# A linear-attention recurrence and an MLP in one instruction stream: a new order of MLP pieces, narrowings and joins

## The chip, the cores and the metric

The kernel runs on one core of one Trainium2 chip. The metric is the device time of one execution in microseconds (us), the median of several runs. Inputs come from and outputs go to HBM.

## The reference

For batch 4, 8 heads, 768 tokens and head size 48, a state of 48 x 48 per head is carried over the tokens (delta rule); then an MLP follows on the 3072 tokens with 384 features:

```python
k_n = k / (norm(k) + 1e-6)
for t in range(S):
    y[:, :, t] = einsum('bhd,bhde->bhe', q[:, :, t], state)
    v_old = einsum('bhde,bhd->bhe', state, kt)
    state = state + bt * einsum('bhd,bhe->bhde', kt, vt - v_old)
x = y.transpose(0, 2, 1, 3).reshape(B * S, H * D)      # 3072 x 384
h = x @ w_in                                            # 384 x 2048
out = (h * sigmoid(h)) @ w_out                          # 2048 x 384
```

The two MLP weights are float64 in HBM and are narrowed to fp32 on the chip with bit operations.

## The kernel before, in words

The 768 tokens are cut into six chunks (c = 0 to 5) of 128, each into two halves of 64 tokens (hf), and the 32 heads into two groups (g). Inside a chunk the recurrence becomes small dense algebra:

- *Scores* (`score`, L530): per head the products k k^T and k q^T within a half, evacuated by ACT and masked by DVE. Their diagonal 32 x 32 blocks go to HBM and come back turned (`block_out` L104, `block_in` L583), so that each of 128 partitions has one block.
- *Inversion* (`invert`, L628 and L633): on DVE, 31 steps per chunk, the triangular factor of all 128 blocks at once. Chunk 0 has its own form (`invert_first`, then `corner`, `turned`, `straight`, `merge_half` on PE, called "the joins", L718 to L807).
- *Factors out*: for chunks 2 to 5 through HBM (`low`, `up`, then xe and xi). For chunk 1 `put_up` (L602) turns the blocks on DVE in place: the first transpose (L606) writes xe, the second (L608) up, and copies make xi of it.
- *Solve* (`solve`): `merge` twice (py and px, L783) joins the 32 x 32 factors to 64 x 64; `keys` (ph, L829) subtracts the old state's part from v; `inner` (pz, L841) applies the factor; `old` (pyc, L909) and `new` (L922) give the outputs; `update` (pu, L861, and L868 on DVE) the next state. The outputs are gathered into xT, some of it by DMA (`move`, L902).
- *MLP*: `hidden` (phid, L1049) with Silu on ACT (L1059) out of two PSUM banks, m0 and m1. For chunk 0 `project` (po, L1084) multiplies by w_out. For the others `combine` (px, py, L1156) does so with sums of quarters of w_out and of the Silu's results (`sum_w` L1120, `sum_g` L1138).
- *Narrowing* (`narrow`, L232 to L245): per piece of 256 rows or columns of a weight, two instructions on ACT ("begin"), then two on DVE, the second with an addition on POOL behind it. w_in has eight pieces (in0 to in7), w_out eight (out0 to out7). The raw float64 data come by DMA (`fetch_w_out`, L306); each of these transfers waits, with `depth`, for the last but one ahead of it on SP's queue.

Every engine runs its instructions in the order in which the program issues them (`pin`), and all loads and stores are in one line on SP (`in_line`). The order is written by hand. For chunks 0 and 1 it is a string of words that `script` reads: `s` one step of `solve`, `j` steps of chunk 0's second joins, `r` one MLP piece (`run`: the next step of `pieces`, after the weight that it needs has been narrowed), `f` one step of a narrowing, `b` the begin of the next one, `p` a step of `prepare` (scores of chunk 1), `i` a step of `invert`, `w3` the load of w_out's raw piece 3, `z` a scaling of v on POOL (`size`), `v` load_v(1), `t` a step of `sum_w`, `m` of the key lengths of chunk 2, `c` all that is left of chunk 0's MLP and then chunk 1's MLP as the next pieces. A piece of `hidden` is three matmuls (six records of PE), one of `project` two, one of `combine` four. For chunks 2 to 5 a loop runs `go(solving)` and then so many pieces from a list.

In the old string chunk 0 has 64 pieces, r1 to r64 below: 16 of hidden(0, 0), 16 of hidden(0, 1), 32 of project.

Of the kernel before, what the change touches and what calls it, by code (L numbers as in the profile page):

```python
# [19 lines left out]
def kernel(  # L20
# [10 lines left out]
    nc = tc.nc  # L31
    B, H, S, D = q.shape
# [4 lines left out]
    NCH = S // C  # L37
# [3 lines left out]
    T = 32  # L41
# [29 lines left out]
    def behind(later, earlier, how=NoSync):  # L71

        tc.add_manual_dep(
            later.ins, earlier.ins.name,
            mybir.DependencyInfo(how, mybir.DependencyReason.DATA), reason="order",
        )
# [3 lines left out]
    def pin(op):  # L80

        engine = op.ins.engine
        if engine in pins:
            behind(op, pins[engine])
        pins[engine] = op
        return op
# [23 lines left out]
    def together(*parts):  # L110
        for _ in zip_longest(*parts):
            pass
# [52 lines left out]
    def in_blocks(c):  # L165

        return 1 < c < NCH
# [142 lines left out]
    def narrow_w_out(i):  # L310
# [14 lines left out]
        out=above[0:W], in_=above[0:W], pattern=[[1, W]], compare_op=ALU.is_gt, fill=0.0,  # L325
# [3 lines left out]
        out=above[W:P], in_=above[W:P], pattern=[[1, W]], compare_op=ALU.is_gt, fill=0.0,  # L329
# [214 lines left out]
    def by_act(to, of):  # L544
        return pin(nc.scalar.copy(to, of))  # L545
# [41 lines left out]
    xes = {}  # L587
# [14 lines left out]
    def put_up(x):  # L602

        both = work.tile([P, BH, T], FP32, name="xe_y", tag="g", bufs=1)
        xes[1], ys[1] = both[:], both[:].rearrange("p (g h) t -> p g h t", g=2)
        pin(nc.vector.transpose(out=both[:].rearrange("p n s -> p s n"), in_=x))  # L606
        up = work.tile([P, BH, T], FP32, name="up_1", tag="x", bufs=1)[:]
        pin(nc.vector.transpose(out=up.rearrange("p n t -> p t n"), in_=x.rearrange("p s t -> p t s")))  # L608
        for j in (1, 3, 0, 2):
            rows, cols = slice(T * j, T * (j + 1)), slice(T * (j % 2), T * (j % 2) + T)  # L610
            for g in range(2):
                of = up[rows, HH * g : HH * (g + 1)]
                if j % 2 == 1 and g == 1:
                    by_act(crossed[T * (4 - j) : T * (5 - j)], of)
                (by_dve if j % 2 == 1 and g == 0 else by_pool if j % 2 == 0 and g == 0 else by_act)(xis[g][rows, :, cols], of)
# [42 lines left out]
    Q, ys = T // 2, {}  # L658
# [177 lines left out]
    def inner(c, g, hf, room=CC):  # L836

        pz = bank(room, "pz")
        for u, p, e, n, _, _ in of_heads():
            rows = on(e, hf, g)  # L840
            yield pin(nc.tensor.matmul(  # L841
                pz[rows, n * D : (n + 1) * D], lhsT=xis[g][rows, u * H + 2 * p + e, :],
                rhs=vfs[c][rows, hf, g * HB + u, p, :], start=True, stop=True,
            ))
        to = zbuf[:, g * HB : (g + 1) * HB, hf, :, 0:D]
        if c == 0 and hf == 0:
            by = (by_act, by_dve) if g == 0 else (by_dve, by_act)
            at = slab[:, g * HB * NP * 2 * D + D :][:, 0 : HB * NP * 2 * D]
            by[0](at.rearrange("p (n w) -> p n w", w=2 * D)[:, :, 0:D], pz[:, 0:DM].rearrange("p (n d) -> p n d", d=D))
            by[1](to, by_heads(pz))  # L850
        else:
            by_act(to, by_heads(pz))
# [23 lines left out]
    def first_outputs(g):  # L876

        pys = [bank(A, f"py{e}") for e in range(2)]
        for u in range(HB):
            for a in range(NKT):  # L880
                for n in range(2):
                    for half in range(2):
                        f = P * a + W * half
                        h = f // D + n
                        p, e = h // 2, h % 2
                        at = ((g * HB + u) * NP + p) * 2 * D + D + f - D * h
                        pin(nc.tensor.matmul(
                            pys[e][HALVES[half], C * a + W * u : C * a + W * (u + 1)],
                            lhsT=slab[on(e, 0, g), at : at + W], rhs=aps[0, g][1][on(e, 0, g), u, h, :],
                            start=True, stop=True,  # L890
                        ))
        xT, half = x_half(0, g, 0)
        to = xT[:, :, half]
        even, odd = (py[:, 0 : NKT * C].rearrange("p (a t) -> p a t", a=NKT) for py in pys)
        by_act(to, even)
        pin(nc.vector.tensor_tensor(out=to, in0=to, in1=odd, op=ALU.add))
# [64 lines left out]
    def copy_out():  # L961
        together(copies.pop(0))
# [18 lines left out]
    def solve(c):  # L981

        if c == 0:
            together(inner(0, 0, 0, CC))
            together(inner(0, 1, 0, M))
            yield
            first_outputs(0)
            yield
            first_outputs(1)
            yield  # L990
            together(update(0, 0, 0), update(0, 1, 0))
            yield
            together(keys(0, 0, 1), keys(0, 1, 1))
            yield
            together(inner(0, 0, 1), old(0, 0, 1))
            yield
            together(inner(0, 1, 1), old(0, 1, 1))
            yield
            together(update(0, 0, 1), update(0, 1, 1))
            yield  # L1000
            together(new(0, 0, 1), new(0, 1, 1))
            copy_out()
            copy_out()
            move()
            yield
            return
        together(merge(c, 0, False), merge(c, 1, False))
        yield
        together(keys(c, 0, 0), keys(c, 1, 0))
        yield  # L1010
        together(merge(c, 0, True), merge(c, 1, True))
        yield
        for hf in range(2):
            if hf == 1:
                together(keys(c, 0, 1), keys(c, 1, 1))
                if c > 1:
                    follow(c)
                yield
            for g in range(2):
                together(inner(c, g, hf), old(c, g, hf))  # L1020
            if hf == 1:
                if c == 1:
                    follow(c)
                load_v(c + 1)
            yield
            made(c, hf)
            yield
            copy_out()
            if hf == 0:
                yield  # L1030
# [348 lines left out]
    corner, turned, straight = next(inv)  # L1379
# [38 lines left out]
    def run(n=1):  # L1418

        for _ in range(n):  # L1420
            name = next(needed, None)
            if name is not None:
                until(name)
            go(pieces)
            begin_soon()
# [121 lines left out]
                pieces = chained(feed_forward(1, 0), feed_forward(1, 1))  # L1547

    for text in (
        "s f s f T f q T s q T j5 j4 j8 j8 f j5 f q r T j20 j5 j8 j4 j16 j5 j4 b r q r f j4 j4 f W7 r b j4 f2 j4 j4 j32 r f e j6 j6 b j8 j4 f j4 j20 f j4 r j4 j99 l h f2 b l s w2 f r2 l p r s l w3 r p r l p f l2 f l3 b l f l2 s l f l p l3 r l3 s l f l r l2 p f s2 l2 H f l4 f r2 f p2 v l g G r i p i p f r i r i2 r i r i b l i r f r i r b r2 i b b b i2 r2 i2 f b i5 r6 f r f r i2 r2 f r i r f r f i4 f i b r2 i3 b f b f r i r i f k r f r z i b r s r2 t z s b r2 b s m2 r5 t f t m f t m2 r s t m r b s b m r m2 s r m r m r c m2 s m r m t b m2 s m2 b m f m2 t r t m3 r m s m",  # L1550
    ):
        script(text)
    for c in range(1, NCH):
        if c > 1:
            solving = solve(c)
            for n in range(9):
                go(solving)
                run(((2, 2, 2, 2, 1, 1, 2, 2, 2), (2, 2, 2, 1, 1, 2, 2, 2, 2))[c == NCH - 1][n])
                if n == 5:
                    pieces = chained(pieces, feed_forward(c, 0), feed_forward(c, 1))  # L1560
        assert next(solving, 0) == 0
        go(long_2, 99)
        if c + 1 < NCH:
            ready = prepare(c + 1)
            for _ in range(3 if c == 1 else 2):
                go(ready)
                run(2)
            step = block_steps(c + 1)
            go(ready)
            run(8 if c > 1 else 6)  # L1570
            for n, _ in enumerate(invert(c + 1, step)):
                run(int(n % 4 != 3 and n != 24))
                if n == 3:
                    load_k(c + 2)
                    if in_blocks(c + 2):
                        load_blocks(k, c + 2, ALL)
            after = lengths(c + 2) if c + 2 < NCH else iter(())
            for _ in range({1: 8, NCH - 2: 10}.get(c, 10)):
                run()
                go(after, 4)  # L1580
            go(after, 99)
# [31 lines left out]
```

## Time and profile before

| | us |
|---|---|
| median of 3 runs (639.11 to 640.27) | 639.91 |
| the profiled execution | 646.08 |
| its span | 644.3 |
| PE busy in it | 623.5 |
| DVE, ACT, POOL busy | 401.2, 217.2, 94.3 |

PE is TensorE (matmuls; PEld its weight loads), DVE VectorE, ACT ScalarE, POOL GpSimd, SP the queue that issues DMAs. L1049 is line 1049 of the kernel. In the lists "x6" counts instruction records; an fp32 matmul gives two. Some records of matmuls are missing in a trace. A row of the chain of waits has the start, the length and what ran. A row of a timeline has the start, the time to the end of the last of the group, the engine, the line, the operation and the tiles, and in brackets the idle time ahead of it with the releaser. PEclk is the granted clock of PE as a share of the full one.

### The profile page before, as it was taken

To read this page: it belongs to the slowest core of one execution; us is meant where nothing else is said; L and a number is where in the kernel's file an instruction comes from. 1 tells how busy PE (TensorE), PEld (TensorE's weight loads), DVE (VectorE), ACT (ScalarE), POOL (GpSimd) and SP (SyncE) were. 2 spreads that over 40 slices of the span, in tenths; PEclk is the share of its full clock that TensorE was granted. 3 is DMA by queue.
4 is the path that set the end of the run, shared out by engine and by line. 5 is a ranking of instruction groups with operands and counts; after the bars stand their busy time and mean duration, and the time that the engine had idled before them with its cause. 6 is when DMAs were issued, how large, how long until landed. Compare 5 with 4: busy or idle time off the path is not lost.

```text
span 644.3 us, 21893 instructions
## 1 busy us (share of the span) xinstructions
PE 623.5 (97%) x9642; PEld 550.1 (85%) x9642; DVE 401.2 (62%) x917; ACT 217.2 (34%) x512; POOL 94.3 (15%) x96
## 2 busy tenths in 40 slices
PE   6879999999999999999999999999999999999997
PEld 4677787756789988999989989989989989889997
DVE  5845688988865986563987563987464974212112
ACT  2655656151342122451122451122451122441120
POOL 5332630237011020010020010020001000000000
PEclk9759799999999999999999999999999999999999
DMA  9755445170278433268434268334173033100101
GB/s 190 164 141 163 146 97 132 50 148 3 58 150 145 62 85 50 54 133 136 70 79 55 47 137 138 69 79 56 26 154 76 9 79 48 40 14 1 25 0 25
DMA packets 141695, 53.69 MB, mean 83 GB/s; under 512 B 113296, under 2 KB 135056, under 8 KB 141600
## 3 DMA queue, kind: packets, MB, share of 16 engines
q1 hardware_dynamic: 141264, 52.14, 40.2%
q8 instruction: 76, 1.25, 0.8%
q10 hardware_dynamic: 336, 0.15, 0.1%
q14 instruction: 19, 0.16, 0.1%
HBM read 39.62 MB, written 10.49 MB: 78 GB/s over the span
## 4 chain that ended last, share of the span: by engine, by line
PE 92%; DMA 2%; issue 2%; DVE 1%; ACT 1%; SPq 1%; POOL 0%; DVEq 0%; POOLq 0%
PE phid L1049 39%; PE px L1156 16%; PE py L1156 12%; PE po L1084 7%; PE pa L530 3%; PE pz L841 2%; PE ph L829 2%; PE pyc L922 2%; PE pu L861 2%; PE pyc L909 2%; PE pt L501 1%; DMA kb<-in_k_dram 1%; DMA xT<-part 1%; PE px L783 1%; PE py L783 1%
## 5 line engine op out<-in xcount | busy, mean ns | idle before, releaser
L1049 PE MATMUL phid<-xT,w_in 128*128 128x256 f32 x1152 | 259.6, 383 | 2.5 <-DMA xT<-part 1.5
L1049 PEld LDWEIGHTS phid<-xT,w_in 128*128 128x128 f32 x1152 | 217.2, 191 | 33.6 <-issue 4.1
L1059 ACT ACTIVATE gT<-phid 128x512 f32<-128x512 f32 x88 | 52.6, 598 | 147.1 <-PE phid L1049 138.5
L628 DVE SCALAR_TENSOR_TENSOR rank<-g,step,x 128x31 f32<-128x31 f32 (+15 forms) x124 | 49.7, 401 | 36.9 <-DMA g<-blocks 33.4
L1138 DVE TENSOR_TENSOR sums_of_g<-gT 128x384 f32<-128x384 f32 (+1 forms) x60 | 29.8, 516 | 56.5 <-ACT gT L1059 46.0
L1156 PE MATMUL py<-w_out,sums_of_g 128*128 128x192 f32 x320 | 56.8, 329 | 0.0
L1156 PE MATMUL px<-sums_of_w,sums_of_g 128*128 128x192 f32 x320 | 56.6, 329 | 0.0
L1156 PEld LDWEIGHTS px<-sums_of_w,sums_of_g 128*128 128x128 f32 x320 | 52.2, 190 | 0.5
L1156 PEld LDWEIGHTS py<-w_out,sums_of_g 128*128 128x128 f32 x320 | 52.2, 190 | 0.4
L633 DVE TENSOR_TENSOR x<-x,rank 128x31 f32<-128x31 f32 (+15 forms) x124 | 42.5, 343 | 4.3
L468 POOL TENSOR_TENSOR vf<-vf,n_slot 128x768 f32<-128x768 f32 x10 | 14.9, 1490 | 167.9 <-DMA vf<-in_v_dram 121.8
L868 DVE TENSOR_TENSOR state<-state,pu 48x384 f32<-48x384 f32 x44 | 24.3, 552 | 21.9 <-PE pu L861 20.9
L545 ACT COPY xT<-pyc 48x128 f32<-48x128 f32 (+2 forms) x126 | 32.7, 260 | 1.7
L489 DVE STREAM_TRANSPOSE kq<-stage 128x512 f32<-128x512 f32 x28 | 28.2, 1112 | 3.9 <-DMA stage<-in_q_dram 3.8
L1156 PE MATMUL px<-sums_of_w,gT 128*128 128x192 f32 x160 | 28.4, 329 | 0.0
L1156 PE MATMUL py<-w_out,gT 128*128 128x192 f32 x160 | 28.4, 329 | 0.0
L1156 PE MATMUL px<-w_out,gT 128*128 128x192 f32 x160 | 28.0, 327 | 0.0
L841 PEld LDWEIGHTS pz<-vf,xi 64*64 64x64 f32 x768 | 25.2, 142 | 3.2 <-issue 2.6
L551 POOL COPY g<-x 64x256 f32<-64x256 f32 x4 | 5.0, 1242 | 152.5 <-DVE x L636 152.5
L1156 PEld LDWEIGHTS px<-w_out,gT 128*128 128x128 f32 x160 | 26.4, 190 | 0.6
L841 PE MATMUL pz<-vf,xi 64*64 64x48 f32 x768 | 26.9, 226 | 0.0
L1156 PEld LDWEIGHTS py<-w_out,gT 128*128 128x128 f32 x160 | 26.1, 190 | 0.3
(197 smaller groups left out, 831.1 us busy)
## 6 DMA issues: line engine op xcount, KB each, us to landing
vf<-in_v_dram SPq DMA_DIRECT2D x48, 96.0 KB, 3.1
out_dram<-o SPq DMA_DIRECT2D x42, 96.0 KB, 2.2
w_out<-in_moe_w_in_dram SPq DMA_DIRECT2D x12, 256.0 KB, 3.5
sums_of_w<-in_moe_w_out_dram SPq DMA_DIRECT2D x8, 384.0 KB, 4.4
blocks<-ap SPq DMA_DIRECT2D x40, 64.0 KB, 1.9
g<-blocks SPq DMA_DIRECT2D x5, 512.0 KB, 3.7
kb<-in_k_dram SPq DMA_DIRECT2D x12, 192.0 KB, 4.4
kb<-in_k_dram SPq DMA_DIRECT2D x24, 96.0 KB, 4.5
```

The lines of the kernel that those rows point to most:

```text
L489: pin(nc.vector.transpose(out=kqs[c, b][:, :, j, :].rearrange("p a (i m) -> p a m i", i=T), in_=src.rearrange("p a (m d) -> p a m d", d=D) ...
L530: pin(nc.tensor.matmul(pa[e][half, p * n * W : (p + 1) * n * W], lhsT=kq[rows, p, 0, half], rhs=kq[rows, p, js[0] : js[-1] + 1, half], sta ...
L545: return pin(nc.scalar.copy(to, of))
L628: pin(nc.vector.scalar_tensor_tensor(out=tv, in0=g[:, 0:m, m : m + 1].to_broadcast([P, m, n]), scalar=step[:, m : m + 1], in1=x[:, m : m + ...
L633: yield pin(nc.vector.tensor_tensor(out=x[:, 0:m, m:T], in0=x[:, 0:m, m:T], in1=tv, op=ALU.add))
L841: yield pin(nc.tensor.matmul(pz[rows, n * D : (n + 1) * D], lhsT=xis[g][rows, u * H + 2 * p + e, :], rhs=vfs[c][rows, hf, g * HB + u, p, : ...
L868: pin(nc.vector.tensor_tensor(out=to, in0=to, in1=by_heads(pu[of]), op=ALU.add))
L1049: pin(nc.tensor.matmul(ph[:, j * GT : (j + 1) * GT], lhsT=w_in[:, a, (2 * f + j) * P : (2 * f + j + 1) * P], rhs=xTs[c, hf][:, a, :], star ...
L1059: pin(nc.scalar.activation(out=hidden_of(c, hf, f), in_=ph[:], func=ACTF.Silu, scale=-0.5 if in_blocks(c) else 0.5))
L1084: pin(nc.tensor.matmul(pos[i][:, 0:DM], lhsT=hidden_of(0, hf, f // 2)[:, at : at + C], rhs=w_outs[f // HFF][:, f % HFF, :], start=(f == 0) ...
L1138: pin(nc.vector.tensor_tensor(out=sums_of_g[:, k, fs], in0=of[0], in1=of[1], op=op))
L1156: pin(nc.tensor.matmul(to, lhsT=at, rhs=quarter(f, *b) if isinstance(b, tuple) else sums_of_w[b][:, f], start=start and f == 0, stop=f == ...
```

## The change

Four things change:

1. `put_up`: the first transpose of chunk 1 writes its result contiguously; xes[1] becomes a view of it with the heads innermost, so that the merge's matmul reads its moving operand with a stride of 32 elements.
2. `solve`: the first merge and the first keys are one step in chunks 1, 2 and 4; in 3 and 5 they stay two.
3. The string: an `r` inside the joins ahead of merge_half(1), one ahead of chunk 0's update (the fourth `s`) with a `b` moved behind it, one `r` fewer behind the update and one fewer between the second and third score; `w3` moved from behind the fifth `s` to ahead of `v`, behind the xT moves; two `r` gathered ahead of the first inversion steps; `z` (the second) ahead of the merge; `c` behind the keys of chunk 1's second half; two `r` fewer behind it.
4. The loop: lists of pieces by chunk (eight entries where the row is shared), and 7 pieces for 6 ahead of chunk 2's inversion.

```diff
     def put_up(x):
         both = work.tile([P, BH, T], FP32, name="xe_y", tag="g", bufs=1)
-        xes[1], ys[1] = both[:], both[:].rearrange("p (g h) t -> p g h t", g=2)
-        pin(nc.vector.transpose(out=both[:].rearrange("p n s -> p s n"), in_=x))
+        turned = both[:].rearrange("p n t -> p (n t)").rearrange("p (s n) -> p s n", s=T)
+        xes[1], ys[1] = turned.rearrange("p s n -> p n s"), both[:].rearrange("p (g h) t -> p g h t", g=2)
+        pin(nc.vector.transpose(out=turned, in_=x))
...
         together(merge(c, 0, False), merge(c, 1, False))
-        yield
+        if c in (3, NCH - 1):
+            yield
         together(keys(c, 0, 0), keys(c, 1, 0))
...
-  j4 j4 f j4 j20 f j4 r j4 j99 l h f2 b l s w2 f r2 l p r s l w3 r p r l p f
+  j4 j4 f j4 j4 r j16 f j4 r j4 j99 l h f2 r l s w2 f r b l p r s l r p l p f
...
-  f r2 f p2 v l g G r i p i p f r i r i2 r i r i b
+  f r2 f p2 w3 v l g G r i p i p r2 f i i2 r i r i b
...
-  k r f r z i b r s r2 t z s b r2 b s m2
+  k r f r z i b z r s r2 t b r2 b s m2
...
-  s r m r m r c m2 s m r m t b m2 s m2 b m f m2 t r t m3 r m s m
+  s r m r m r m2 s c m t b m2 s m2 b m f m2 t r t m3 m s m
...
             solving = solve(c)
-            for n in range(9):
+            counts = {
+                2: (4, 3, 2, 1, 1, 2, 2, 2), 3: (2, 2, 2, 2, 1, 1, 2, 2, 2),
+                4: (2, 4, 2, 1, 1, 2, 2, 2), 5: (2, 2, 2, 1, 1, 2, 2, 2, 2),
+            }[c]
+            for n, count in enumerate(counts):
                 go(solving)
-                run(((2, 2, 2, 2, 1, 1, 2, 2, 2), (2, 2, 2, 1, 1, 2, 2, 2, 2))[c == NCH - 1][n])
-                if n == 5:
+                run(count)
+                if n == len(counts) - 4:
                     pieces = chained(pieces, feed_forward(c, 0), feed_forward(c, 1))
...
-            run(8 if c > 1 else 6)
+            run(8 if c > 1 else 7)
```

The lines of the string are shown as the stretches that differ, with their words in the kernel's order.

More of the change, by code (lines that the diff above doesn't have):

```diff
@@ L1549 @@
     for text in (
-        "s f s f T f q T s q T j5 j4 j8 j8 f j5 f q r T j20 j5 j8 j4 j16 j5 j4 b r q r f j4 j4 f W7 r b j4 f2 j4 j4 j32 r f e j6 j6 b j8 j4 f j4 j20 f j4 r j4 j99 l h f2 b l s w2 f r2 l p r s l w3 r p r l p f l2 f l3 b l f l2 s l f l p l3 r l3 s l f l r l2 p f s2 l2 H f l4 f r2 f p2 v l g G r i p i p f r i r i2 r i r i b l i r f r i r b r2 i b b b i2 r2 i2 f b i5 r6 f r f r i2 r2 f r i r f r f i4 f i b r2 i3 b f b f r i r i f k r f r z i b r s r2 t z s b r2 b s m2 r5 t f t m f t m2 r s t m r b s b m r m2 s r m r m r c m2 s m r m t b m2 s m2 b m f m2 t r t m3 r m s m",
+        "s f s f T f q T s q T j5 j4 j8 j8 f j5 f q r T j20 j5 j8 j4 j16 j5 j4 b r q r f j4 j4 f W7 r b j4 f2 j4 j4 j32 r f e j6 j6 b j8 j4 f j4 j4 r j16 f j4 r j4 j99 l h f2 r l s w2 f r b l p r s l r p l p f l2 f l3 b l f l2 s l f l p l3 r l3 s l f l r l2 p f s2 l2 H f l4 f r2 f p2 w3 v l g G r i p i p r2 f i i2 r i r i b l i r f r i r b r2 i b b b i2 r2 i2 f b i5 r6 f r f r i2 r2 f r i r f r f i4 f i b r2 i3 b f b f r i r i f k r f r z i b z r s r2 t b r2 b s m2 r5 t f t m f t m2 r s t m r b s b m r m2 s r m r m r m2 s c m t b m2 s m2 b m f m2 t r t m3 m s m",
     ):
```

## The prediction, on record before the changed kernel ran

> **What bounds the kernel now.** The page of the profile comes first: the engine that is busy nearly all the span, and the clock that it was granted.
>
> ```profile
> span 644.3 us, 21893 instructions
> PE 623.5 (97%) x9642; PEld 550.1 (85%) x9642; DVE 401.2 (62%) x917; ACT 217.2 (34%) x512; POOL 94.3 (15%) x96
> PEclk9759799999999999999999999999999999999999
> ```
>
> PE is the bound. The MLP pieces fill whatever the recurrence leaves open, and the last of them ends the span. So a change of order can win only three things: idle time of PE, time at a low clock, and the small cost of going from one kind of matmul to another. The list of waits of PE shows where idle time is left behind the start:
>
> ```profile
> PE px L807 <- issue: 1.6, 1, 1.6
> PE phid L1049 <- DMA xT<-part: 1.5, 2, 1.3
> PE phid L1049 <- issue: 1.0, 1, 1.0
> ```
>
> Three waits of 1.6, 1.3 and 1.0 us. "Issue" is a wait for which the profile shows no releaser. The busy time by stretch, cut where the clock changes, shows what the first one brings with it (columns: span, PE busy, PEld, DVE, ACT, POOL, PEclk, DMA share, GB/s):
>
> ```profile
> 62.78:66.20 3.42, 3.42 (x169) 2.89 (x169) 3.21 (x5) 3.20 (x6) 1.85 (x1) 1.00 0.65 198
> 66.20:69.61 3.41, 1.82 (x45) 1.56 (x42) 2.24 (x4) 3.05 (x6) 1.35 (x1) 1.00 0.14 48
> 69.61:73.02 3.41, 3.41 (x110) 2.70 (x111) 1.25 (x3) 1.86 (x4) 1.25 (x2) 0.50 0.56 148
> 73.02:76.44 3.42, 3.42 (x35) 2.79 (x28) 3.33 (x7) 2.85 (x4) 3.42 (x5) 0.50 0.66 207
> 76.44:79.85 3.41, 3.41 (x48) 2.47 (x47) 2.38 (x4) 1.22 (x3) 2.46 (x3) 1.00 0.38 115
> ```
>
> The stretch from 66.20 has 1.82 us of PE in 3.41 us. Right behind it PE runs at half clock for 6.83 us, which loses 3.4 us. The chain of work around it:
>
> ```profile
> 66.74 1.59 issue
> 68.33 0.28 PE px L807 x5
> 68.60 1.84 PE phid L1049 x6
> 70.44 1.64 PE px L807 x56
> 72.08 1.46 PE pu L861 x64
> 73.54 4.24 PE phid L1049 x12
> 77.78 0.62 PE pa L530 x32
> 78.40 1.49 PE phid L1049 x6
> ```
>
> A piece ("r" in the order's text) is six phid matmuls, 1.49 us behind small tiles. At half clock two of them took 4.24.
>
> **The change part by part.** I number the chunk-0 pieces r1 to r64 as the order's text runs them; their number doesn't change.
>
> *The joins and the update.* r6 goes between straight(1) and merge_half(1), ahead of the gap; r8 goes ahead of the update (pu), r9 behind it. The gap is worth between nothing (it moves along with PE) and 1.59. I take that its end at 68.33 stands, as nothing of PE is named as its releaser: the 1.49 of r6 go into it, **1.5 us gained**. The stretch 66.20:69.61 then has 1.82 + 1.49 = 3.3 us of PE, as the neighbours at 1.00 have (3.42, 3.41). So I take the half clock as gone: between 0 and 3.4 us, taken **3.4 us**. PE is 4.9 us ahead at this place, with nothing else in the way.
>
> There is something in the way, by two routes. The rows:
>
> ```profile
> 74.67 2.27 DVE L868 TENSOR_TENSOR state<-state,pu 48x384 f32<-48x384 f32 x4
> 78.01 1.84 POOL L245 TENSOR_TENSOR w_in<-w_in,w_out 128x768 int32<-128x768 int32 x1 [0.95 <-DVE w_in L241]
> 82.40 0.69 PE L530 MATMUL pa<-stage 48*64 48x64 f32 x32
> 84.51 0.69 PE L530 MATMUL pa<-stage 48*64 48x64 f32 x32
> 83.81 1.94 SPq L104 DMA_DIRECT2D blocks<-ap  x4
> 94.78 0.34 SPq L583 DMA_DIRECT2D g<-blocks  x1
> 95.17 4.13 SPq L902 DMA_DIRECT2D xT<-part  x5
> 98.70 2.70 DMA xT<-part
> ```
>
> PE's new order from 68.33: px 0.3, r7 1.5, px 0.8 (half of 1.64), r8 1.5, pu 0.7 (half of 1.46), r9 1.5, pa 0.6, r10 1.5, keys 1.1 (the ph row further down), so r11 could start at 77.8. r11 is the first to read w_in piece 5, which POOL finishes (78.01 + 1.84) behind the state sums on DVE. With pu done at 73.1 the sums can start some 1.2 us sooner than 74.67 (I let DVE keep 0.4 us for what stands ahead of them), so the piece is there at 79.85 - 1.2 = 78.7, and r11 waits 0.9 us. The second score of chunk 1 (the pa at 82.40) now stands behind r11 and no longer behind r10: it starts at 78.7 + 1.5 = 80.2, **2.2 us earlier and not 4.9**. From it hangs a run on SP's queue that PE can't shorten: the blocks out (83.81), a weight load, the blocks again, g<-blocks (94.78), the five xT moves (95.17 for 4.13), landed at 101.40. All of that moves by 2.2, so xT lands at 99.2. PE, 3.6 us ahead behind the next score (the piece between the two scores is gone: 80.2 + 0.7 = 80.9 against 84.51), comes to r17 at 100.2 (its wait of 1.3 ended with the landing) - 3.6 = 96.6 and waits 2.6 us instead of 1.3. What is late next is thus the xT wait, and **2.2 us is what is left of the 4.9**. The ends: 4.9, if the moves come sooner than I think, and 0.
>
> *w3 behind the xT moves.* In the old order w3 is issued at 73.72 and long there when ACT reads it at 106.62; now it stands behind the moves and w4, and ahead of load_v(1).
>
> ```profile
> 73.72 1.67 SPq L306 DMA_DIRECT2D sums_of_w<-in_moe_w_out_dram  x2
> 99.96 1.80 SPq L306 DMA_DIRECT2D sums_of_g<-in_moe_w_out_dram  x2
> sums_of_w<-in_moe_w_out_dram SPq DMA_DIRECT2D x8, 384.0 KB, 4.4
> 106.62 0.91 ACT L232 ACTIVATE w_out<-sums_of_w 128x768 f32<-128x768 f32 x1
> ```
>
> Each such transfer waits for the last but one ahead of it (depth). With w4 2.2 earlier (97.8 and 99.6) and 4.4 us to land, w3's second half is issued at 104.0 and lands at 108.4. ACT wants it at 106.62 - 2.2 = 104.4. ACT then stands for 4.0 us, and behind it stand the Silus. PE has two phid banks and so about four pieces (5.2 us, from 103.9) before it stands too; the Silu that frees the bank ends at 108.4 + 1.9 + 0.6 = 110.9 against 109.1. That is 1.8 us; landings one us shorter each make it nothing. I take **0.7 us lost**, ends 0 and 1.8. load_v(1) behind it is late by some 4 us and is first read by "z", behind all of invert(1).
>
> *One row for merge and keys, chunks 1, 2, 4.* What a switch costs is in these rows:
>
> ```profile
> 243.46 1.22 PE py L783 x82
> 244.67 2.80 PE px L1156 x16
> 247.47 1.10 PE ph L829 x64
> 627.83 2.60 PE py L1156 x16
> ```
>
> Sixteen wide matmuls take 2.80 behind small tiles and 2.60 behind wide ones. A row less is a switch less: 0.2 us each. Behind the merge ACT and DVE copy y; two to four pieces stand ahead of the second merge, so that wait is covered. Chunks 2 and 4 give **0.4 us**. That the same bursts back to back could outrun the issue of instructions (1.0 to 1.6 us, the "issue" rows) I keep for the range.
>
> *Chunk 1's factors.* put_up's first transpose now writes contiguously:
>
> ```profile
> L1301 DVE STREAM_TRANSPOSE sums_of_w<-blocks 128x1024 f32<-128x1024 f32 x1 | 1.2, 1250 | 0.0
> 135.25 2.04 DVE L606 STREAM_TRANSPOSE xe_y<-sums_of_w 128x1024 f32<-128x1024 f32 x1
> 141.29 1.22 PE py L783 x82
> ```
>
> The nearest row with a contiguous result is 1.25 us against 2.04: DVE gains 0.8 us. It is off the path: the merge starts 4 us behind the transpose, and PE has project pieces until then. In return the merge reads its factor at a stride of 128 bytes. No row shows a strided read by PE. Its cost lies between nothing and 0.8 us (1.22 times the ratio of the two transposes, less 1.22). I take nothing, as the strides of DVE's two transposes are on the written side and not the read one. The Trainium skill, SBUF — State Buffer, "Door 1: The DMA port swizzle", speaks against this edit: reads that use one fp32 of each 16-byte line pay for it. By that rule the sum would be up to 0.8 us worse; the trace has only DVE's written side to hold against it, which agrees.
>
> *The rest.* Narrowing 7 begun behind r9, out2 behind r18, and "z" ahead of the merge move work of ACT and POOL by a piece or two, beside project or phid pieces; if that cover were gone, each would cost its own 1.5 to 1.9 us. At the end of chunk 1 two phid pieces go behind the last join of states, project's last two behind the keys, and the issue wait of 1.0 us may go. But chunk 2's merge has its own bound:
>
> ```profile
> 239.64 0.93 SPq L651 DMA_DIRECT2D xe<-low  x2
> xe<-low SPq DMA_DIRECT2D x8, 128.0 KB, 2.3
> ```
>
> Its factor lands at 239.64 + 0.93 + 2.3 = 242.9, only 0.6 us ahead of the merge at 243.46. PE now comes there with one piece (1.3 us) fewer behind it, so what it gains at chunk 1's end it waits for here: **nothing** net, ends 1 us either way.
>
> *The sum:* -2.2 + 0.7 - 0.4 = -1.9 us. The profiled execution took 646.08 us (1.8 outside its span of 644.3), 6.2 above the median of 639.91. I carry the difference over in us: 639.91 - 1.9 = **638.0 us**. About 0.2% (1.3 us) is what a measurement of this kernel can tell from no change.
>
> **The rivals.**
>
> *A: the clock falls again (slower).* Place: the xT wait at r17, 96.6 to 99.2. A wait of 2.6 us leaves at most 0.8 us of PE in a stretch of 3.41, when 1.82 was enough for half clock at 69.61. Price: two stretches at half clock, 3.4 us, as at 69.61: -1.9 + 3.4 = +1.5, 641.4 us. It decides from an idle time of about 1.6 us in one stretch; where the stretches begin decides whether the wait is split. Against it: the 1.3 us wait at r17 left the clock alone (9 in every slice of the PEclk row behind the fourth).
>
> *B: the half clock was not the gap's doing (no change).* It then stays, r6 wins 1.5 and the second score, now one piece (1.5) later in the order, eats that at xT. Left are +0.7 and -0.4: 640.2 us. The Trainium skill, TensorE: Matmul & The Clock Gate, "Why this matters for your kernels", asks only for no idle gaps above about 3 us, and by it 1.59 us would not cost the clock. For A and against B: the stretch ahead of the half clock is the only one of the five rows in which PE idles.
>
> *C: the xT run is not the bound.* Then the 4.9 remain: 639.91 - 4.9 - 0.4 + 0.7 = 635.3 us.
>
> **How the numbers follow.** Forecast 0.52 (its own range 636.5 to 638.6: w3's two ends and the 0.4), A 0.19, B 0.21, C 0.08. Left out at the ends is half of C and the worst of A with the strided read (0.8) on top. The range is 635.2 to 641.5. Faster by over 0.2%: the forecast's part below 638.6 (0.49) and C, 0.57; slower: A, most of it, and a little of B, 0.19; within: 0.24.
>
> **What would show it.** Right: no "issue" row at px, clock 1.00 from 60 to 96; the second score near 80; the xT wait at 2 to 3 us; ACT's read of w3 waiting for a DMA near 104; the transpose near 1250 ns; ph next to py in chunks 1, 2 and 4. Wrong: a half clock near 70 (B) or near 100 (A); the chunk 1 merge well above 1.22 (stride); xT landed before PE asks (C); a new idle row inside a merged row.

## The result, and the profile after

The changed kernel takes 645.92 us (median of 16 runs, 642.74 to 650.81), the kernel before 640.04 us on the same chip (16 runs, 638.95 to 644.69). The ratio, taken over all these runs, is 1.0083, 95% interval 1.006 to 1.0106 (the two medians alone would give 1.0092): **slower by 0.8%**, where 0.3% faster was forecast; the forecast's range ended at 641.5.

The profiled execution shown ahead of the prediction (646.08 us) is longer than any of the 16 runs of that kernel, and has a stretch at half clock near 70 us that a second look at the same kernel, 640.31 us, does not have. The second look is the better one to compare with. Its span, its clock, and then its waits of PE:

```profile
span 638.5 us, 21893 instructions
...
PEclk9759999999999999999999999999999999999999
```

```profile
PE px L807 <- issue: 1.4, 1, 1.4
...
PE phid L1049 <- DMA xT<-part: 0.7, 2, 0.5
```

The same two views of the changed kernel (its lines count one or two higher: L807 is L808, L1049 is L1051):

```profile
span 644.3 us, 21892 instructions
...
PEclk9869999999999998999999999999999999999999
```

```profile
PE phid L1051 <- DMA xT<-part: 2.9, 3, 1.7
...
PE phid L1051 <- ACT kq L1061: 1.2, 1, 1.2
...
PE py L784 <- DMA xe<-low: 1.0, 2, 0.5
PE phid L1051 <- POOL w_in L245: 0.7, 1, 0.7
...
PE py L808 <- issue: 0.6, 1, 0.6
```

The gap in front of px (1.4) is nearly gone. In its place stand the longer wait for xT (0.7 to 2.9; the first profile of the kernel before had 1.5), a wait for a Silu (ACT kq, 1.2), one for weight piece in5 (POOL w_in, 0.7) and one for chunk 2's factor (xe, 1.0). The clock has an 8 in its 16th slice (from 241.6), where chunk 2's merge is. Where the first three cost, the chain of waits of the changed kernel shows in order of time:

```profile
73.83 1.86 POOL w_in L245
75.73 1.56 PE phid L1051 x6
...
94.39 2.88 DMA xT<-part
97.30 5.16 DMA sums_of_g<-in_moe_w_out_dram
102.47 3.41 DMA sums_of_w<-in_moe_w_out_dram
...
106.78 1.01 ACT sums_of_w L233
107.79 0.48 ACT kq L1061
108.31 10.63 PE phid L1051 x48
```

r11 (75.73) waits for in5, as forecast, and the second score stands behind it. From 94.39 the chain is no longer PE's: xT's moves, w4's load, w3's load, the narrowing of w3 on ACT, a Silu, and only then PE. Busy time of PE in the same stretch, the kernel before (second look) and then the changed one:

```profile
60.00:120.00 60.00, 57.81 (x1075) 47.12 (x1074) 52.54 (x116) 34.75 (x67) 21.04 (x16) 1.00 0.45 122
```

```profile
60.00:120.00 60.00, 54.08 (x987) 44.05 (x981) 50.80 (x114) 33.94 (x66) 20.93 (x16) 1.00 0.43 118
```

PE does 3.7 us less in these 60 us. More is lost at chunk 2's merge (chain, then busy time by stretch, of the changed kernel):

```profile
238.37 2.64 DMA xe<-low
...
241.06 1.25 PE py L784 x80
...
243.73 2.77 PE phid L1051 x6
```

```profile
239.50:242.90 3.40, 2.45 (x174) 1.94 (x174) 2.99 (x13) 0.52 (x1) 0.00 (x0) 0.99 1.32 163
242.90:246.30 3.40, 3.40 (x42) 2.85 (x33) 3.26 (x14) 0.64 (x2) 0.00 (x0) 0.50 0.76 86
```

PE waits 1.0 us for xe, then does the merge and the keys in one row, and has half clock for 3.4 us (six phid records take 2.77 instead of 1.49).

### The profile page after: what moved, and what is told of

Read it like the earlier page. It is cut to its first block, busy times and chain, and to the rows that moved or that the text cites. A ratio compares the mean times of both kernels' runs of the same rounds, so it can differ in the third digit from the quotient of the medians.

```text
span 644.3 us, 21892 instructions
## 1 busy us (share of the span) xinstructions
PE 620.4 (96%) x9642; PEld 546.9 (85%) x9642; DVE 403.7 (63%) x917; ACT 216.9 (34%) x512; POOL 94.9 (15%) x96
## 3 DMA queue, kind: packets, MB, share of 16 engines
q8 instruction: 76, 1.25, 0.8%
## 4 chain that ended last, share of the span: by engine, by line
PE 79%; DVE 9%; DMA 7%; issue 2%; ACT 1%; SPq 1%; POOL 1%; DVEq 0%; POOLq 0%; ACTq 0%
PE phid L1051 31%; PE px L1158 14%; PE py L1158 11%; PE po L1086 7%; PE pz L842 2%; PE pa L530 2%; DVE rank L629 2%; DVE x L634 2%; PE pyc L923 2%; PE ph L830 2%; PE pyc L910 2%; PE pu L862 1%; DMA stage<-in_q_dram 1%; DMA kb<-in_k_dram 1%; DMA xT<-part 1%
## 5 line engine op out<-in xcount | busy, mean ns | idle before, releaser
L1051 PE MATMUL phid<-xT,w_in 128*128 128x256 f32 x1152 | 259.5, 383 | 4.8 <-DMA xT<-part 2.9
L1051 PEld LDWEIGHTS phid<-xT,w_in 128*128 128x128 f32 x1152 | 216.7, 191 | 36.1 <-issue 3.5
```

The source lines that it names most:

```text
L1051: pin(nc.tensor.matmul(ph[:, j * GT : (j + 1) * GT], lhsT=w_in[:, a, (2 * f + j) * P : (2 * f + j + 1) * P], rhs=xTs[c, hf][:, a, :], star ...
```

## The experiments

My theory after the result: the losses add up from three places that the forecast had as gains, as nothing or as little (the joins part, w3, and the wait for xe at chunk 2's merge), and the half clock that the forecast wanted to win was chance. The main rival: one part does all of it.

Each run below was timed beside the kernel before, whose median there was 640.9 to 642.3 us, so the ratios are to be compared and not the medians. A trace shows one execution, which lay up to 4.3 us above its kernel's median (the gap alone) and up to 2.5 below it (the transpose alone), so only waits and distances are read from it. "..." in an edit stands for what is left out.

**The kernel before, looked at again** (no edit).

> The kernel before, unchanged, for a second profile. The profiled execution of before took 646.08 us, 6.0 above the median of its 16 runs (640.04), and the changed kernel's median is 645.92. If the half clock near 70 us (6.8 us long, 3.4 us lost) was a chance of that one profile, this profile shows a time near 640 and no half clock between 60 and 90. If it is the rule, the time is near 640 all the same and the half clock stands, and the 6 us lie elsewhere.

Measured: 640.31 us, one execution, shown above. The gap in front of px is 1.4 us here too, and no half clock follows it. So the gap alone does not bring the half clock, and in an execution at the median the 3.4 us that the forecast took from it are not there to be won.

**The joins and the update alone.**

```
-  j4 f j4 j20 f j4 r j4 j99 l h f2 b l s w2 f r2 l p r s l w3 r p r l p f
+  j4 f j4 j4 r j16 f j4 r j4 j99 l h f2 r l s w2 f r b l p r s l w3 r p l p f
```

> Before, with the pieces of the joins and the update alone (r6 between straight(1) and merge_half(1), r8 ahead of the update with the begin of narrowing 7 behind r9, one piece fewer between scores two and three; w3 stays where it was). The forecast's step: 2.2 us faster. The rival: PE now waits for weight piece 5 from POOL and the xT run behind the second score starts a piece later than it did in a typical execution of before: 1 to 3 us slower.

Measured: 642.23 us, ratio 1.0029 (1.0008 to 1.005). Its waits of PE:

```profile
PE phid L1049 <- ACT w_out L232: 1.8, 1, 1.8
PE phid L1049 <- POOL w_in L245: 0.7, 1, 0.7
```

The gap of 1.4 us and the wait for xT (0.7) are gone, and 2.5 us of new waits are there, for narrowings on ACT and for in5. This part is slower by itself, as the rival has it; the wait for ACT stood in neither text.

**w3 alone**, behind the xT moves.

```
-  l p r s l w3 r p r l p f    ...    f r2 f p2 v l g G
+  l p r s l r p r l p f       ...    f r2 f p2 w3 v l g G
```

> Before, with w3 alone moved behind the xT moves. In the changed kernel's trace the chain of waits runs through two weight loads (97.3 to 105.9 us), ACT's narrowing and its Silu to the phid at 108.3. Theory late load: 1.2 to 3 us slower, with ACT waiting for the w3 transfer near 104 us. Rival (the load is hidden by the phid banks): within 0.5 us of before.

Measured: 643.71 us, ratio 1.0043 (1.0022 to 1.0065). Its chain:

```profile
97.30 4.53 DMA sums_of_g<-in_moe_w_out_dram
...
101.85 3.32 DMA sums_of_w<-in_moe_w_out_dram
...
106.06 1.03 ACT sums_of_w L233
```

The chain of loads and narrowing of the changed kernel is here with nothing but w3 moved. ACT waits 2.6 us for the load in this run and 3.4 in the changed kernel.

**The changed kernel with the old first transpose.**

```
-  turned = ...
-  pin(nc.vector.transpose(out=turned, in_=x))
+  pin(nc.vector.transpose(out=both[:].rearrange("p n s -> p s n"), in_=x))
```

> The changed kernel with the old first transpose of chunk 1 (strided on the written side, contiguous for the merge). Theory stride: the merge falls back from 1.93 us to 1.22 and the time from 645.9 by about 0.7 to 645.2. Rival (the merge's length is covered by the wait at chunk 2's merge): no change, 645.9.

Measured: 646.05 us, ratio 1.0094 (1.0061 to 1.0126), not to be told from the changed kernel's. The merge takes 1.29 us again, and the wait for xe at chunk 2's merge is 1.4 us instead of 1.0, which fits the rival; the theory's 0.7 us less lies within the interval too.

**The tail alone**: rows merged in chunks 1, 2 and 4, the lists of pieces, z, c and s moved, 7 pieces ahead of chunk 2's inversion.

```
+  if c in (3, NCH - 1):
       yield
...
-  k r f r z i b r s r2 t z s b r2 b s m2    ...    t m3 r m s m
+  k r f r z i b z r s r2 t b r2 b s m2      ...    t m3 m s m
...
-  run(8 if c > 1 else 6)
+  run(8 if c > 1 else 7)
```

> Before with the tail of the change alone: merge and keys in one row in chunks 1, 2 and 4, the lists of pieces by chunk, z, c and s moved, two pieces fewer at the end of chunk 1 and 7 for 6 ahead of chunk 2's inversion; joins, w3 and the first transpose of chunk 1 as before. Theory T (what the parts before 120 us don't explain of the loss arises at chunk 2's merge: PE comes there with one piece fewer behind it, waits 1.0 us for xe and runs at half clock for 3.4 us behind it, 1.7 us lost): +2.5 us less 0.4 of the rows, about +2 us (ratio 1.003 to 1.004), with the wait of py for xe of 0.5 to 1.5 us near 238 us and PEclk below 1.00 in the slice behind it. Rival N (the recorded forecast's step: nothing net at chunk 2's merge): -0.4 us, 0.9994, no xe wait of over 0.3 us, clock 1.00. Rival I (the wait for xe needs the 3 us that joins and w3 put ahead of it): as N in time, and xe issued near 234.4 as in before.

Measured: 642.25 us, ratio 1.0018 (0.9997 to 1.0039). Its wait of PE:

```profile
PE py L783 <- DMA xe<-low: 0.9, 2, 0.5
```

The wait for xe is there without the 3 us that joins and w3 put ahead of it, so T has the wait right and rival I falls. The half clock did not come with it, so T's 2 us were too many; 1.2 is the measured middle, and the interval just holds no change.

**The changed kernel with w3 back in its old place.**

```
-  l p r s l r p l p f       ...    f r2 f p2 w3 v l g G
+  l p r s l w3 r p l p f    ...    f r2 f p2 v l g G
```

> After with w3 where it stood in before (issued behind the fifth score, ahead of the xT moves); all else as in after. Theory S (parts add): the wait of ACT for w3 of 3.4 us at 102 to 106 goes, chunk 1's merge starts about 1 to 2 us sooner than after's 138.6 and the time is 1 to 3 us below after's (ratio to before 1.004 to 1.007). Rival O (joins and w3 hide in each other, since both hold the same Silus near 105 us): no change to after, ratio 1.008 to 1.009, the chain near 95 us running through narrowings of out pieces on ACT as in the run with the joins alone.

Measured: 644.87 us, ratio 1.0057 (1.0026 to 1.0088), inside S's span and below O's, though the interval reaches into O's. The chain shows no load of w3 any more; PE goes from xT straight to its pieces:

```profile
96.26 2.01 DMA xT<-part
...
98.40 20.09 PE phid L1051 x92
```

**Rows merged in chunks 2 and 4 alone.**

```
+        if c in (1, 3, NCH - 1):
             yield
...
+  2: (4, 2, 2, 1, 1, 2, 2, 2), 4: (2, 4, 2, 1, 1, 2, 2, 2)
```

> Before with merge and keys in one row in chunks 2 and 4 alone; the pieces between them go behind the row (4 ahead of the second merge), their sum stays 16. Theory R (a row less is one switch of matmul shape less, 0.2 us each): -0.4 us, ratio 0.9994, which the interval can hardly tell from 1. Rival K (the row of 128 small tiles behind a landing xe takes PE's clock to half for 3.4 us by itself): +1.5 us, 1.0023, PEclk below 1.00 in the slices around 238 us.

Measured: 642.13 us, ratio 1.0021 (0.9994 to 1.0049). R's gain isn't seen: its value lies at the very end of the interval. K's number (1.0023) is met, but not by K's way, as PEclk is 1.00 there. What is new stands in the waits of PE, in chunk 4:

```profile
PE px L783 <- DVE y L548: 0.8, 1, 0.8
```

With merge and keys in one row, DVE has fewer pieces of PE in which to copy y, and the second merge (px) waits for it. From chunk 4's merge to its first update the traces with two rows take 16.7 us in six of eight and 16.9 and 17.0 in the others, 16.8 on average; those with one row take 16.5 to 17.6, 17.0 on average of seven.

**The changed kernel with chunk 2's row apart.**

```
-        if c in (3, NCH - 1):
+        if c in (2, 3, NCH - 1):
...
-  2: (4, 3, 2, 1, 1, 2, 2, 2)
+  2: (2, 2, 3, 2, 1, 1, 2, 2, 2)
```

> After with chunk 2's first merge and first keys apart again, two pieces between them (2, 2, 3 in place of 4, 3). Theory H (the half clock behind chunk 2's merge comes of the xe wait together with the 2.5 us of small tiles right behind it): with two pieces behind the merge the clock stays at 1.00, the xe wait of 1.0 stays, and the time is 1.5 us (1.7 less 0.2 for one switch more) below after's, ratio 1.006. Rival W (the wait alone takes the clock): half clock as in after, and 0.2 us above after's, ratio 1.0095.

Measured: 645.52 us, ratio 1.0067 (1.0037 to 1.0097): H's number, with the clock at 1.00 behind chunk 2's merge, but the interval holds the changed kernel's 1.0083 too, and the wait for xe was only 0.4 in this run. It stays open.

**Only the gap filled.**

```
-  j4 f j4 j20 f j4 r j4 j99 l h f2 b l s w2 f r2 l p
+  j4 f j4 j4 r j16 f j4 r j4 j99 l h f2 b l s w2 f r l p
```

> Before with one edit: one of the two MLP pieces behind chunk 0's update goes into the joins, between straight(1) and merge_half(1), where PE stands 1.4 us in front of px. The number of pieces ahead of each score stays, so that the second score stays behind the piece that doesn't read weight piece in5 (in the changed kernel it stands behind the one that does). Theory J (filling the gap is worth it; what costs time in the joins part is the further piece ahead of the update, which brings the reader of in5 ahead of the second score and moves scores, blocks and xT late against PE): the issue wait at px falls below 0.6 us, no wait of PE for w_in of over 0.3 us, second score near 76.2 us instead of 77.6, chunk 1's merge 1 us sooner than 135.9, time -1.0 us (ratio 0.998). Rival G (the gap in front of px moves along with PE, it is a wait in the supply of instructions): the same issue wait ahead of px or one place later, time within 0.3 us of before (1.000). Rival L (PE ahead of the xT moves: the wait for xT grows by what the gap gave): xT wait 2 us, time 1.000.

Measured: 642.01 us, ratio 1.0013 (0.9988 to 1.0038). Its waits of PE:

```profile
PE phid L1049 <- DMA xT<-part: 2.6, 1, 2.6
PE pa L530 <- DVE state L868: 1.2, 1, 1.2
```

The gap is gone and in5 is not waited for, so it isn't the reader of in5 alone. J falls: now the first score waits for DVE's state sums, and PE for xT, as L had it. DVE's order of time tells why. The kernel before (second look), the changed one, and this run; the third row of the first two is POOL's in5 and the fourth the second score:

```profile
68.45 0.98 DVE L548 COPY xi<-px 32x256 f32<-32x256 f32 x2 [1.83 <-PE px L807]
71.52 2.27 DVE L868 TENSOR_TENSOR state<-state,pu 48x384 f32<-48x384 f32 x4
74.86 1.86 POOL L245 TENSOR_TENSOR w_in<-w_in,w_out 128x768 int32<-128x768 int32 x1 [0.95 <-DVE w_in L241]
77.58 0.69 PE L530 MATMUL pa<-stage 48*64 48x64 f32 x32
```

```profile
67.43 0.98 DVE L548 COPY xi<-px 32x256 f32<-32x256 f32 x2 [1.62 <-PE px L808]
70.49 2.27 DVE L869 TENSOR_TENSOR state<-state,pu 48x384 f32<-48x384 f32 x4
73.83 1.85 POOL L245 TENSOR_TENSOR w_in<-w_in,w_out 128x768 int32<-128x768 int32 x1 [0.95 <-DVE w_in L241]
77.23 0.79 PE L530 MATMUL pa<-stage 48*64 48x64 f32 x34
```

```profile
72.69 0.98 DVE L548 COPY xi<-px 32x256 f32<-32x256 f32 x2 [1.55 <-PE px L807]
75.76 2.27 DVE L868 TENSOR_TENSOR state<-state,pu 48x384 f32<-48x384 f32 x4
```

From the copy of px to the state sums are 3.07, 3.06 and 3.07 us; to in5 on POOL 6.41 and 6.40 (the runs differ in when they come here, so only the distances are compared). This run on DVE and POOL has no slack: it doesn't get shorter because PE stands a piece further. The second score is 9.1 us behind the copy in the kernel before and 9.8 in the changed one.

**The tail with 8 pieces ahead of chunk 2's inversion**, one fewer behind its row.

```
-  run(8 if c > 1 else 7)      2: (4, 3, 2, 1, 1, 2, 2, 2)
+  run(8)                      2: (4, 2, 2, 1, 1, 2, 2, 2)
```

> The tail part alone once more, but with 8 pieces for 7 ahead of chunk 2's inversion and one fewer behind chunk 2's row (4, 2, 2 in place of 4, 3, 2), so that chunk 2's merge has as many pieces ahead of it as in before. Theory T (PE meets the wait for xe because it comes with one piece fewer): no wait of py for xe of over 0.3 us near 237 us, and the time 0.9 us below that of the tail alone (ratio to before 0.9995 to 1.001). Rival D (the inversion itself, ranking and gather on DVE and POOL, runs later in the new order whatever PE has to do): the xe wait stays at 0.5 us or more, ratio 1.0018 as with the tail alone.

Measured: 642.23 us, ratio 1.0011 (0.9988 to 1.0034). No wait for xe is left in this trace, as T says and against D. The time can't be told from that of the tail alone, and between chunk 1's merge and chunk 2's first update PE stands in other places instead:

```profile
PE pa L530 <- ACT ap L545: 0.8, 1, 0.8
PE pa L530 <- DVE kq L489: 0.7, 1, 0.7
```

**The new first transpose alone.**

```
+  turned = both[:].rearrange("p n t -> p (n t)").rearrange("p (s n) -> p s n", s=T)
+  xes[1] = turned.rearrange("p s n -> p n s")
-  pin(nc.vector.transpose(out=both[:].rearrange("p n s -> p s n"), in_=x))
+  pin(nc.vector.transpose(out=turned, in_=x))
```

> Before with the new first transpose of chunk 1 alone. Theory P (PE pays for the strided read, and nothing covers it): the transpose takes 1.25 us instead of 2.04, the merge of chunk 1 1.9 us instead of 1.22, and everything behind it moves by 0.7 us: ratio 1.001, from merge to first update 21.2 us instead of 20.5. Rival E (DVE's gain of 0.8 us is worth as much elsewhere): merge 1.9 us, but merge to first update as before, ratio 1.000.

Measured: 643.03 us, ratio 1.0025 (1.0006 to 1.0045), P's side. PE's order of time in this run (merge, first update), and then in the kernel before:

```profile
135.78 2.00 PE L784 MATMUL py<-xe_y,ap 32*32 32x32 f32 x128
...
156.99 0.94 PE L862 MATMUL pu<-z,kb 64*48 64x48 f32 x64
```

```profile
135.86 1.29 PE L783 MATMUL py<-xe_y,ap 32*32 32x32 f32 x128
...
156.35 0.94 PE L861 MATMUL pu<-z,kb 64*48 64x48 f32 x64
```

The merge with the strided operand takes 0.71 us more, and the first update behind it is 0.7 us later against the merge's start (21.21 for 20.49). Nothing covers it, while the 0.8 us that DVE saves lie ahead of the merge, beside project pieces, and show no gain. Of the 1.6 us that 0.25% are, the trace thus shows 0.7; the interval (0.4 to 2.9 us) holds that.

**The joins, with in5's narrowing ahead of the update.**

```
-  l h f2 r l s w2 f r b l p
+  l h f2 r f l s w2 r b l p
```

> The joins part alone, but with the narrowing step of in5 (the f behind w2) ahead of chunk 0's update instead of behind it. Theory J: DVE and POOL finish in5 some 2 us sooner, the wait of phid for POOL's w_in (0.7 us) goes, the second score comes 0.7 us sooner than the 78.9 us of the joins alone, and the time falls by 0.5 to 0.7 us against it (ratio to before 1.002 for 1.003). Rival U (in5 doesn't matter, the order of the pieces against the xT moves and the narrowing of out pieces on ACT does): the in5 wait goes but PE stands as much longer for ACT's w_out or for xT near 95 us, ratio 1.003.

Measured: 644.04 us, ratio 1.0053 (1.0035 to 1.0072): not faster than the joins alone (1.0029, to 1.005), and above both theories' numbers. The wait for in5 is gone, but the narrowing now stands ahead of the state sums, 4.2 us behind the copy instead of 3.1, and the first score waits for them:

```profile
PE pa L530 <- DVE state L868: 0.9, 1, 0.9
```

**The gap filled, and DVE's narrowing behind the state sums.**

```
-  j99 l h f2 b l s w2 f r l p
+  j99 l h f b l s w2 f2 r l p
```

> The run with the gap filled (one piece from behind the update into the joins) with one step more: DVE's narrowing of 1.0 us that stands between px's copies and the state sums goes behind the sums. Theory Q (from px on, a fixed run on DVE sets the way to the scores and xT: copies, narrowing, sums of squares, state, and the piece in the gap only brings PE sooner to the waits behind it): the wait of the first score for DVE's state falls from 1.2 to 0.2 us, the second score comes about 7.1 us behind DVE's last copy from px instead of 8.1, xT lands 1 us sooner against it, and the time is 1 us below that of the gap run (1.0013), ratio 0.9997. Rival X (the run on ACT, SP and the DMAs behind the scores sets xT, not the scores): the wait for the state goes, but the wait for xT grows by as much, ratio 1.0013.

Measured: 642.2 us, ratio 0.9995 (0.9966 to 1.0024): near Q's number, but the interval holds X's too, and it did not come by Q's way. The wait for the state stays at 1.0 us: with the narrowing out of the way, DVE's sums of squares wait for POOL (its order of time):

```profile
70.21 0.55 DVE L389 TENSOR_REDUCE ss<-sq 128x8 f32<-128x384 f32 x1 [0.54 <-POOL sq L385]
...
71.58 2.26 DVE L868 TENSOR_TENSOR state<-state,pu 48x384 f32<-48x384 f32 x4
```

So the state sums are held twice, by DVE's queue and by POOL's sq behind it, and taking away the one shows the other. In this run no wait for xT is left, for a reason that the trace doesn't name. Sums of squares behind the state sums were not tried.

## Why the prediction was wrong

**The parts add up, as far as can be told.** Joins +0.29%, w3 +0.43%, tail +0.18% (its interval holds nothing), the transpose +0.25%: 1.15% with an uncertainty of some 0.4 for the sum, against 0.83% (0.60 to 1.06) for all together. No part is faster, and no one part does it.

**The half clock near 70 (3.4 us to be won): wrong, and this is the first step that failed.** I took one profiled execution for the kernel. The second look has the same gap and no half clock. The quoted execution was 6 us above the median, and I carried that over as a constant instead of asking what it consisted of. Rival B, with a chance of 0.21, had it right that closing the gap wins no clock, and that the second score then comes later; by it alone the time would have been 640.2. Whether the gap has a part in the half clock stays open: of the five traces with 1.1 us or more of it, two have half clock behind it (the quoted one and the tail with 8 pieces), of the ten others none.

**The second score (2.2 us earlier, all that was left of the 4.9): the same half clock again.** From the start of the state sums to the second score are 7.73 us in the quoted execution (82.40 less 74.67), 6.06 in the second look and 6.74 in the changed kernel. The forecast has 6.7 for the changed kernel (80.2 less 73.5), so the new order was read rightly. What was wrong is the order that it was compared with: in the quoted execution the two pieces ahead of the first score took 4.24 us at half clock, in the second look 2.79. The other 1.2 of the 2.2 us, the sums that start sooner, are also half clock: px and the piece ahead of it were let end 1.15 us sooner (1.64 cut to 0.8, 1.84 to 1.5). The sums hang on the copy of px, 3.06 us behind it in either order, by a run on DVE that PE can't shorten. Taken from the second look, the forecast's own chain has the second score 0.7 us later and not 2.2 earlier.

**The gap filled by r6 (1.5 us to be won): half of it, and not kept.** The issue row at px went from 1.4 to 0.6 and below. But the gap isn't the same in every execution: the seven traces with the old joins have 1.6, 1.4, 1.3, 1.1, 1.1, 0.6 and none. From the burst of pl (L747) ahead of the gap to the second burst of px are 3.1 to 4.4 us in the five of them without half clock there, 3.9 on average, and 4.3 to 5.2 in the eight with r6, 4.6 on average: r6's 1.5 us cost 0.7 of PE's time there. What PE is ahead it waits out at in5 (0.7, forecast 0.9) and at xT (2.9, forecast 2.6). The first is there in all five traces with the joins and the update as changed. The second is in part luck: of the same five traces one has no wait for xT, the others 1.5 to 2.9, and the landing scatters against the second score (see what stays open).

**w3: the step is right, its size is not.** The stop of ACT was forecast at 4.0 us and measured at 3.4 (2.6 with w3 alone). I charged 0.7 of it, with 1.8 as the worst end. Measured alone it is 0.43% (0.22 to 0.65), that is 2.8 us (1.4 to 4.2). The trace shows only part of it: PE waits 0.5 for the Silu and 0.4 for the narrowing, 0.9 us in all and near the 0.7 charged, and po starts 1.1 to 1.9 us later against the copy of px (49.5 for 47.7, 47.7 and 48.4 in three runs with nothing changed up to there). The wait for xT is longer too, 1.4 for 0.7, but the two executions of the kernel before differ as much. Taking w3 back out of the change gives 0.26%, with intervals that overlap.

**One row for merge and keys (0.4 us to be won): not seen.** "Two to four pieces stand ahead of the second merge, so that wait is covered" failed: px waits 0.2, 0.4 and 0.8 us for y in three of the seven kernels with a merged row in chunk 4 (and 0.6 us for a result that ACT writes in a fourth), and merge to update takes 17.0 us there on average against 16.8 with two rows, not the 16.5 of the changed kernel that one switch less gives against 16.7.

**The strided operand (taken at nothing): wrong end of its bounds.** 0.71 us was measured of 0 to 0.8, and the transpose alone makes the kernel slower by 0.25%. The row that I named nearest, DVE's 1.25 for 2.04, was the right measure: the stride of 128 bytes costs PE 0.71 us on reading, and DVE's transpose with a strided result takes 0.8 us more. (Undone in the changed kernel it wins nothing that the interval shows: 1.0094 for 1.0083.) The Trainium skill, SBUF — State Buffer, "Door 1: The DMA port swizzle", had warned of strided fp32 reads, and the trace agrees in kind (1.29 to 2.00 us).

**Chunk 2's merge (nothing, 1 us either way): its bad end came true.** The factor landed after PE asked: 1.0 us of wait in the changed kernel, 0.9 with the tail alone, none with one piece more ahead of it (and 0.4 and 0.5 in two runs with the old tail). To it comes, in some executions, a half clock.

**Rival A in another place.** It put a half clock at the xT wait, from 1.6 us of idle time. There the clock stayed at 1.00, even with 2.6 us of wait (the gap alone). It fell behind the wait for xe, at 1.0 us, where a row of small tiles follows. It isn't most of the loss: of the 16 runs of the changed kernel the eight with a mean clock of 0.978 or more have a mean span of 643.4 us and the other eight 644.8. (The 9s of the PEclk row that were held against A begin behind the fifth slice, not the fourth: the fifth, a 7, is the half clock near 70.)

**The signs.** Nearly all that were named for "right" came: clock 1.00 from 60 to 96, an xT wait of 2.9, ACT's wait for w3 near 104, the transpose at 1.24 us, ph next to py. (Of those for "wrong" one came: the strided merge at 2.00 us.) They tell what the new order does, and none of them tells what the old one took without the half clock.

**What stays open:** where the part of w3's loss lies that PE's waits don't show, why the gap and the half clock differ from one execution to the next, why the runs behind the second score differ by up to 3 us in the time to xT's landing (17.2 us behind it with the transpose alone, 20.4 with the gap filled) with no edit between the two, and whether filling the gap alone is worth anything (1.0013 and 0.9995, both intervals hold 1).

## What to carry to other kernels

Before a stretch at low clock is counted as a gain, look at a second execution: the one here, 1% above the median, had 6.8 us at half clock that the second look lacked, and the rows behind it were late by it, so that a gain was read from them too. An idle gap of the busiest engine is worth filling only if the work behind the gap is not fed by another engine's run; measure the distance from the gap's first result to the next wait in the other engines' order of time, and if it has no slack the gap only moves. A load that is moved later has to be costed with everything queued behind its reader, and an operand's layout by its reader on the path, not by its writer off it.

## What the runs showed of the hardware

- Half clock doesn't go by PE's idle time alone. Two runs had nearly the same stretch in front of px, 2.07 and 2.08 us busy of 3.40; behind the first, the tail with 8 pieces, the clock fell for 3.4 us, behind the second, the kernel before, it didn't. In the run with w3 back it fell behind a stretch without any idle time, in which small tiles with the strided operand ran; behind the same merge it did not in the three other traces with that operand:

```profile
137.90:141.30 3.40, 3.40 (x194) 3.07 (x194) 1.15 (x3) 3.33 (x6) 1.99 (x2) 0.99 0.69 236
141.30:144.70 3.40, 3.40 (x6) 1.86 (x6) 3.30 (x7) 1.94 (x3) 0.48 (x1) 0.50 0.02 5
```

  Waits for xe of 0.4 (twice), 0.5 and 0.9 us were followed by full clock, those of 1.0, 1.3 and 1.4 by half clock (merge and keys in one row in the last four of these seven). The Trainium skill, TensorE: Matmul & The Clock Gate, "Why this matters for your kernels", speaks of idle gaps above about 3 us; these traces show half clock behind less.
- A matmul of 32x32 whose moving operand has a stride of 128 bytes goes at 15.6 ns apart instead of 10.1 (2.00 and 1.29 us for 128).
